# A cap of three on the loads under way at the start of a fused attention, MLP and expert kernel

## The chip, the cores and the metric

The kernel runs on one core of one Trainium2 chip. The metric is the device time of one execution in microseconds (us). TensorE (PE in the profile, with PEld for its weight loads) does the matmuls, VectorE (DVE), ScalarE (ACT) and GpSimd (POOL) the elementwise work, and SyncE (SP) issues nearly all transfers. The transfers of the core run on 16 DMA engines.

## The reference, cut to what matters

Three stages follow each other on an input of 2 sequences of 768 tokens and 8 heads of 64. The first is a decayed linear attention ("retention"), which carries a 64 by 64 state per head from block to block.

```python
def _attn_ref(q, k, v, lam):
    ...
    for b in range(nb):
        ...
        intra = np.einsum('bhic,bhjc->bhij', qb, kb) * Dmask[None]
        intra = np.einsum('bhij,bhjd->bhid', intra, vb)
        inter = np.einsum('bhid,bhde->bhie', qb * lam_pow[None], kv_state)
        out[:, :, sl] = intra + inter
        ...
        kv_state = lam_block[None, :, None, None] * kv_state + np.einsum('bhsd,bhse->bhde', kb_dec, vb)

def _moe_ref(x, g_ln, w_ch1, w_ch2):
    ...
    xn = (x - mu) / np.sqrt(var + 1e-06) * g_ln
    ch = np.maximum(xn @ w_ch1, 0.0) @ w_ch2
    return (x + ch).astype(np.float32)
```

The last stage is a mixture of 4 experts: each is a causal softmax attention with one head of 64, and each token keeps its two best. The layer norm and MLP (512 to 2048 and back) work on 1536 tokens, and so does the last stage. All inputs are float32.

## The kernel before, in words

The retention stage takes the 2 sequences in 12 chunks of 128 tokens. Chunk `n` needs two loads of 512 KB each: `qk` (q and k, transposed, `load_qk`, line 119) and `kvn` (k and v, `load_kv`, line 128). Every fourth chunk's loads go into a borrowed tile called `early`; the others rotate through three buffers, so a load also waits until the chunk that used its buffer is done. Between them the queue gets the first MLP weights, `raw`, 512 KB each (`load_w`, line 139; one of them goes to `early` too).

PE's order in this stage is written by hand. For each chunk it runs, in this order: the scores of the next chunk (`sc`, line 340, needs that chunk's `qk`), the old state's part of the output (`po<-qd,st`, line 385), the state update (`ps`, line 375, needs `kvn` and its decayed copy `kd`), and the inner part of the output (`po<-a,kvn`, line 392). DVE multiplies the scores by the decay (`a`, line 361) and sums the state (`st`); POOL makes `qd`, `kd` and `old`; ACT copies the output to `xT`. From the third chunk on, pieces of the layer norm (`mu`, `mean`, `dq`, `xn`), of weight splitting (`mag`, `top`, `w`) and later of the MLP (`h`, line 514) are put between. After the twelfth chunk the kernel is a long row of MLP and attention matmuls.

SP issues the transfers in program order, one queue, and an issue that waits holds up all issues behind it. Transfers take turns over eight semaphores. Before the change a load waits only for its buffer and for the transfer eight places in front of it, whose semaphore it takes over.

The profile's DMA queue q8, of kind "instruction", carries packets that are not loads of the kernel: 28 of them, 0.46 MB.

Of the kernel before, what the change touches and what calls it, by code (L numbers as in the profile page):

```python
# [11 lines left out]
I32 = mybir.dt.int32  # L12
# [19 lines left out]

W_SLOTS = ((4, 6), (4, 8))
WARM = (10, 3)

ROOM = (1.5, 3.0)
ROOM_MLP = 1.5
# [31 lines left out]
def model(ctx, tc, qkT, kv, lam, g_ln, w12, wat, out):  # L69
    nc = tc.nc  # L70
# [19 lines left out]
    def ps_big(name):  # L90
        return psum.tile([P, 2, 512], F32, tag="big", bufs=2, name=name)
# [10 lines left out]
    def warm(n, name):  # L102
        ps = ps_mid(f"warm{name}")
        for _ in range(n):
            nc.tensor.matmul(ps, zeros[:, :P], zeros, start=True, stop=True)

    warm(WARM[0], "a")

    R = {}

    early = xnp.tile([P, 3, 1024], F32, tag="xn", name="early")

    def load_qk(n):
        b, c = order[n]
        if n % 4 == 3:
            qk = early[:, 0].rearrange("p (a h i) -> p a h i", a=2, h=HP)
        else:
            qk = r2.tile([P, 2, HP, P], F32, tag="qk", name=f"qk{b}{c}", bufs=3)
        nc.sync.dma_start(qk, qkT[b, c])
        R.setdefault((b, c), {})["qk"] = qk  # L120

    def load_kv(n):
        b, c = order[n]
        if n % 4 == 3:
            kvn = early[:, 1].rearrange("p (a h d) -> p a h d", a=2, h=H)
        else:
            kvn = r2.tile([P, 2, H, D], F32, tag="kvn", name=f"kvn{b}{c}", bufs=3)
        nc.sync.dma_start(kvn, kv[b, c])
        R.setdefault((b, c), {})["kvn"] = kvn

    RAW = {}

    def load_w(ft, i):

        if (ft, i) == (2, 0):
            raw = early[:, 2].bitcast(I32).rearrange("p (c two) -> p c two", two=2)
        else:
            raw = stage.tile([P, 512, 2], I32, tag="raw", name=f"raw{ft}_{i}")
        nc.sync.dma_start(raw, w12[ft, :, i * 512:(i + 1) * 512].bitcast(I32)
                          .rearrange("p (c two) -> p c two", two=2))  # L140
        RAW[ft, i] = raw

    WRAW = []
# [43 lines left out]
    while rest:  # L187
        for p in rest:
            ft, i = p
# [5 lines left out]
        else:  # L195
            p = None
# [5 lines left out]
        assert n < len(steps), rest  # L202
    pieces = first + [plan[n] for n in sorted(plan)]
    to_load = [lambda p=p: load_w(*p) for p in pieces] + [lambda i=i: load_wa(i) for i in range(4)]

    def load_next(k=1):
# [76 lines left out]
    for k in (0, 1):  # L283
        load_qk(k)
    load_kv(0)
    g_sb = const.tile([P, KT], F32, tag="g", name="g_sb")
    nc.scalar.dma_start(g_sb, g_ln)
# [20 lines left out]
    for h in range(H):  # L308
        nc.vector.tensor_tensor_scan(dec[:, h, :], lq[:, h:h + 1].to_broadcast([P, P]), hit, 0.0, ALU.mult, ALU.add)
    load_kv(1)  # L310
    load_qk(2)
    load_next()
    load_kv(2)
    load_qk(3)

    for h2 in range(2):
# [18 lines left out]
    def ret_scores(n):  # L335
        r = R[order[n]]
        sc = r["sc"] = ps_big(f"sc{n}")
        for hp, h2 in HEADS:
            for kh in range(2):
                nc.tensor.matmul(sc[half(kh), h2, cols(hp)], r["qk"][half(h2), 1, hp, half(kh)],  # L340
                                 r["qk"][half(h2), 0, hp, :], start=True, stop=True, skip_group_check=True)

    def ret_qd(n):
        b, c = order[n]
        if c > 0:
            r = R[b, c]
            r["qd"] = r2.tile([P, HP, P], F32, tag="qd", name=f"qd{n}")
            nc.gpsimd.tensor_tensor(r["qd"], r["qk"][:, 0], qpow, ALU.mult)

    def ret_decay(n):  # L350
        b, c = order[n]
        r = R[b, c]
        if c < NC - 1:
# [14 lines left out]
    def ret_state(n):  # L368

        b, c = order[n]  # L370
        r = R[b, c]
        if c < NC - 1:
# [5 lines left out]
    def ret_outer(n):  # L378
        b, c = order[n]
        r = R[b, c]  # L380
        r["po"] = ps_big(f"po{n}")
        if c > 0:
            st = ST.pop(n - 1)
            for hp, h2 in HEADS:
                nc.tensor.matmul(out_at(r["po"], hp, h2), st[half(h2), hp, :], r["qd"][half(h2), hp, :],
                                 start=(hp < 2), stop=False, skip_group_check=True)
# [253 lines left out]
    while n < len(order) or min(norm_at) < 3 or norm_parts or weight_parts:  # L640
        if n < len(order):
# [8 lines left out]
            if n == 0:  # L650
                warm(WARM[1], "b")
            ret_outer(n)
# [276 lines left out]
    for k in range(len(items) + LAG + O_AT + 1):  # L929
        if k < len(items):  # L930
            b, t, e = items[k]
# [7 lines left out]
        i = k - 1  # L939
        if 0 <= i < len(items):  # L940
            att_c(*items[i])
        i = k - LAG
        if 0 <= i < len(items):
            att_t(*items[i])
        i = k - LAG - AV_AT
        if 0 <= i < len(items) and items[i][2] % 2 == 1 and i < len(items) - 1:
            b, t, e = items[i]
# [3 lines left out]
        i = k - LAG - O_AT  # L951
# [56 lines left out]
```

## Time and profile before

| what | value |
|---|---|
| median of 3 runs | 467.2 us (466.13 to 467.33) |
| profiled execution, time | 466.95 us |
| its span, first to last instruction | 465.2 us |
| PE busy | 453.3 us, 97% of the span |
| PE's granted clock | full in every slice |
| DMA, mean over the span | 91 GB/s |
| DMA in the second slice of 40 (11.6 to 23.3 us) | 409 GB/s, busy share 9 tenths or more |

The span is what the trace covers; the 1.75 us between it and the profiled time lie around it. An engine's busy time counts its own instructions; idle time before an instruction is given with what ended it.

### The profile page before, as it was taken

What the parts mean: (1) busy time and instruction counts of PE and PEld (TensorE: products, weight loads), DVE (VectorE), ACT (ScalarE), POOL (GpSimd) and SP (SyncE); (2) the same over time, 40 slices, a digit from 0 to 9 for tenths busy, and PEclk for the clock granted to TensorE, in tenths of its full rate; (3) what the DMA queues carried; (4) which work ended last, traced back from release to release, by engine and by line L of the source; (5) the groups of instructions that cost most, each with busy time, mean ns of one, the idle gap of its engine ahead of it and who ended that gap; (6) DMA issues with size and microseconds to landing.
All of it is one profiled execution on the core that took longest, in us unless ns stands there. A gap on an engine that the chain in (4) does not pass through costs nothing.

```text
span 465.2 us, 9098 instructions
## 1 busy us (share of the span) xinstructions
PE 453.3 (97%) x3562; PEld 421.0 (91%) x3563; DVE 334.6 (72%) x698; ACT 208.5 (45%) x476; POOL 86.6 (19%) x132
## 2 busy tenths in 40 slices
PE   8789999999999999999999999999999999999997
PEld 4666779999999999999999999999998898998885
DVE  5887988869778778537789745646788686586663
ACT  3568675445433213113225311311466666557673
POOL 6745500000000000000000000000055443344340
PEclk9999999999999999999999999999999999999999
DMA  7997115634421222101224412220000000001011
GB/s 281 409 359 269 48 61 190 197 90 135 138 91 50 87 92 77 60 0 47 90 92 129 155 35 51 56 65 1 0 1 0 25 25 24 23 2 38 33 45 70
DMA packets 15226, 42.33 MB, mean 91 GB/s; under 512 B 2240, under 2 KB 5072, under 8 KB 15184
## 3 DMA queue, kind: packets, MB, share of 16 engines
q1 hardware_dynamic: 14896, 41.62, 26.3%
q8 instruction: 28, 0.46, 0.4%
q10 hardware_dynamic: 288, 0.13, 0.1%
q14 instruction: 14, 0.11, 0.1%
HBM read 35.43 MB, written 6.32 MB: 90 GB/s over the span
## 4 chain that ended last, share of the span: by engine, by line
PE 73%; DVE 8%; ACT 3%; issue 1%; POOL 0%; ACTq 0%; DVEq 0%
PE y L548 27%; PE h L514 23%; PE s L844 5%; PE av L893 4%; PE t L881 4%; PE o L914 4%; PE pj L764 3%; PE pv L786 3%; DVE qs L772 1%; PE yf L570 1%; DVE kl L776 1%; DVE w L255 1%; ACT att L856 1%; DVE xn L454 0%; ACT xn L451 0%
## 5 line engine op out<-in xcount | busy, mean ns | idle before, releaser
L514 PE MATMUL h<-xn,w 128*128 128x384 f32 x768 | 139.8, 336 | 0.0
L514 PEld LDWEIGHTS h<-xn,w 128*128 128x128 f32 x768 | 133.4, 188 | 2.8 <-issue 0.8
L548 PE MATMUL y<-hs,w 128*128 128x384 f32 x552 | 99.7, 334 | 0.0
L548 PEld LDWEIGHTS y<-hs,w 128*128 128x128 f32 x552 | 96.1, 188 | 0.0
L533 ACT ACTIVATE hs<-h 128x384 fp32r<-128x384 f32 x50 | 24.5, 490 | 108.6 <-PE h L514 99.0
L778 POOL TENSOR_SCALAR kh<-kh 64x384 fp32r<-64x384 f32 x16 | 8.1, 507 | 293.1 <-ACT kh L775 291.3
L534 DVE SCALAR_TENSOR_TENSOR hs<-h,hs 128x384 fp32r<-128x384 f32 x50 | 27.7, 554 | 34.6 <-ACT hs L533 34.5
L871 POOL TENSOR_SCALAR att<-att,c,gw 128x128 f32<-128x128 f32 (+5 forms) x48 | 35.6, 747 | 51.9 <-DVE c L868 16.0
L556 DVE TENSOR_TENSOR xT<-xT,y 128x768 f32<-128x768 f32 x24 | 22.8, 951 | 28.3 <-PE y L548 28.3
L243 ACT CAST w<-top 128x512 fp32r<-128x512 f32 x32 | 19.9, 621 | 42.3 <-DVE top L237 42.3
L764 PE MATMUL pj<-x,wa 128*128 128x384 f32 x192 | 35.0, 337 | 0.0
L764 PEld LDWEIGHTS pj<-x,wa 128*128 128x128 f32 x192 | 33.3, 188 | 0.0
L882 ACT COPY aT<-t 128x512 f32<-128x512 f32 (+3 forms) x64 | 26.5, 441 | 11.2 <-PE t L881 11.0
L881 PE MATMUL t<-ident,att 128*128 128x128 f32 x168 | 26.2, 275 | 0.5 <-DVE qs L772 0.5
L252 DVE TENSOR_TENSOR top<-top,w 128x512 f32<-128x512 f32 x32 | 24.0, 750 | 0.0
L893 PE MATMUL av<-aT,v 128*64 128x128 f32 x336 | 23.7, 280 | 0.0
L844 PE MATMUL s<-kh,qs 128*128 128x512 f32 (+3 forms) x64 | 23.3, 365 | 0.0
L248 DVE SCALAR_TENSOR_TENSOR mag<-raw,mag 128x512 f32<-128x512 uint32 x31 | 22.6, 729 | 0.7
L237 DVE SCALAR_TENSOR_TENSOR top<-raw,mag 128x512 int32<-128x512 int32 x31 | 22.2, 718 | 0.5
L228 ACT ACTIVATE mag<-raw 128x512 f32<-128x512 f32 x31 | 20.5, 669 | 4.2 <-DVE w L255 2.1
L255 DVE TENSOR_TENSOR w<-top,mag 128x512 fp32r<-128x512 f32 x32 | 21.9, 684 | 0.4
L893 PEld LDWEIGHTS av<-aT,v 128*64 128x64 f32 x336 | 18.0, 136 | 4.2 <-issue 3.5
(137 smaller groups left out, 702.1 us busy)
## 6 DMA issues: line engine op xcount, KB each, us to landing
raw<-in_w SPq DMA_DIRECT2D x31, 512.0 KB, 3.7
qk<-in_qkT SPq DMA_DIRECT2D x9, 512.0 KB, 6.5
kvn<-in_kv SPq DMA_DIRECT2D x9, 512.0 KB, 6.7
xd<-xT SPq DMA_DIRECT2D x4, 768.0 KB, 4.4
xr<-xd SPq DMA_DIRECT2D x8, 384.0 KB, 3.2
out<-os SPq DMA_DIRECT2D x11, 256.0 KB, 2.0
early<-in_qkT SPq DMA_DIRECT2D x3, 512.0 KB, 8.6
early<-in_kv SPq DMA_DIRECT2D x3, 512.0 KB, 4.6
```

The source lines that it names most:

```text
L252: nc.vector.tensor_tensor(t["top"], t["top"], t["w"][:, 0].bitcast(F32), ALU.subtract)
L255: nc.vector.tensor_tensor(t["w"][:, 1], t["top"], t["mag"], ALU.add)
L514: nc.tensor.matmul(ph[:, :TB], w[:, wi, k, :], xn[:, xi, k, :], start=(i == 0), stop=(i == 11))
L533: LAST.append((nc.scalar.activation(h[:, 0], ph[:, :TB], AF.Relu), nc.vector.scalar_tensor_tensor(h[:, 1], ph[:, :TB], 0.0, h[:, 0].bitcas ...
L534: nc.vector.scalar_tensor_tensor(h[:, 1], ph[:, :TB], 0.0, h[:, 0].bitcast(F32), ALU.max, ALU.subtract)))
L548: nc.tensor.matmul(y[:, j, :TB], w[:, wi, e * P:(e + 1) * P], h[:, xi], start=(f == 0 and i == 0), stop=(f == GF - 1 and i == 2))
L764: nc.tensor.matmul(ps[:, :TB], w[:, wi, k, :], x2[:, xi, k, :], start=(i == 0), stop=(i == 11))
L844: nc.tensor.matmul(ps[:, c0:c1], q, kk[:, e, c0:c1], start=(i == 0), stop=(i == 1))
L871: nc.gpsimd.tensor_scalar(a[:, :n], a[:, :n], c, gw, ALU.mult, ALU.mult)
L881: nc.tensor.transpose(pt[:, (j - j0) * P:(j - j0 + 1) * P], a[:, j * P:(j + 1) * P], ident)
L882: nc.scalar.copy(aT[:, j0 * P:j1 * P], pt[:, :(j1 - j0) * P])
L893: nc.tensor.matmul(pav[e2 * HD:(e2 + 1) * HD, pr * P:(pr + 1) * P], v[:, j, e * HD:(e + 1) * HD], row["aT"][e][:, j * P:(j + 1) * P], star ...
```

## The change

`load_qk` and `load_kv` issue through a new function `load`, and so does `load_w` while fewer than 28 loads have gone through it. `load` keeps the issued loads in a list; from the fourth on, each gets a dependency on the one three places in front of it, so SP waits for that one's landing before it issues.

```diff
+IN_FLIGHT = 3
+N_HELD = 28
...
+    FLYING = []
+
+    def load(dst, src):
+
+        t = nc.sync.dma_start(dst, src)
+        if len(FLYING) >= IN_FLIGHT:
+            tc.add_manual_dep(t.ins, FLYING[-IN_FLIGHT].name,
+                              mybir.DependencyInfo(mybir.DependencyClass.Sync, mybir.DependencyReason.DATA),
+                              reason="in flight")
+        FLYING.append(t.ins)
...
-        nc.sync.dma_start(qk, qkT[b, c])
+        load(qk, qkT[b, c])
...
-        nc.sync.dma_start(kvn, kv[b, c])
+        load(kvn, kv[b, c])
...
-        nc.sync.dma_start(raw, w12[ft, :, i * 512:(i + 1) * 512].bitcast(I32)
-                          .rearrange("p (c two) -> p c two", two=2))
+        (load if len(FLYING) < N_HELD else nc.sync.dma_start)(
+            raw, w12[ft, :, i * 512:(i + 1) * 512].bitcast(I32).rearrange("p (c two) -> p c two", two=2))
```

No instruction moves on any engine; only SP's waits change. Here are SP's issues from the fifth instruction on, before the change. The number after a tile's name is its buffer; a wait on `DMAHW2` is one for the transfer that used that semaphore last.

```order
4 L128 DMA kvn_117<-in_kv 128x1024
5 L128 DMA kvn_154<-in_kv 128x1024
6 L119 DMA qk_156<-in_qkT 128x1024
7 L139 DMA raw_0_158<-in_w 128x1024
8 L128 DMA kvn_160<-in_kv 128x1024 [waits DMAHW0_49]
9 L119 DMA early<-in_qkT 128x1024 [waits DMAHW1_49]
10 L128 DMA early<-in_kv 128x1024 [waits DMAHW2_49]
11 L119 DMA qk_203<-in_qkT 128x1024 [waits DMAHW3_49,PE_49]
12 L128 DMA kvn_263<-in_kv 128x1024 [waits PE_49,DMAHW4_49,Activation_49,Pool_49]
13 L119 DMA qk_265<-in_qkT 128x1024 [waits DMAHW5_49,Pool_49]
```

The first nine transfers wait for nothing that takes long; the tenth (number 10) waits for the first `qk`, eight places in front. The same issues after the change:

```order
4 L116 DMA kvn_117<-in_kv 128x1024
5 L116 DMA kvn_154<-in_kv 128x1024 [waits DMAHW2_49]
6 L116 DMA qk_156<-in_qkT 128x1024 [waits DMAHW3_49]
7 L116 DMA raw_0_158<-in_w 128x1024 [waits DMAHW4_49]
8 L116 DMA kvn_160<-in_kv 128x1024 [waits DMAHW5_49,DMAHW0_49]
9 L116 DMA early<-in_qkT 128x1024 [waits DMAHW6_49,DMAHW1_49]
10 L116 DMA early<-in_kv 128x1024 [waits DMAHW7_49]
11 L116 DMA qk_203<-in_qkT 128x1024 [waits DMAHW0_49,PE_49]
12 L116 DMA kvn_263<-in_kv 128x1024 [waits PE_49,DMAHW1_49,Activation_49,Pool_49]
13 L116 DMA qk_265<-in_qkT 128x1024 [waits DMAHW2_49,Pool_49]
```

Number 5 now waits for number 2, number 6 for number 3, and so on up to the 29th load, number 31; the waits for buffers (PE, ACT, POOL) stay. Numbers 2 to 4 go out as before. In what follows "load 9" means the load with that number.

## Rows read from the trace of the kernel before

**Rows 1.** Page: busy time by engine, and the instruction queue's packets, MB, share.

```profile
PE 453.3 (97%) x3562; PEld 421.0 (91%) x3563; DVE 334.6 (72%) x698; ACT 208.5 (45%) x476; POOL 86.6 (19%) x132
...
q8 instruction: 28, 0.46, 0.4%
```

**Rows 2.** Windows of 6 us: busy per engine (count), PE clock, DMA share, GB/s.

```profile
6.00:12.00 6.00, 5.38 (x130) 4.17 (x127) 3.85 (x6) 2.73 (x9) 4.80 (x8) 1.00 1.03 414
...
24.00:30.00 6.00, 6.00 (x133) 4.31 (x136) 3.83 (x7) 3.28 (x8) 3.86 (x4) 1.00 1.00 375
```

**Rows 3.** Timeline of SP, 0 to 45 us: start, duration, issue.

```profile
1.19 0.88 SPq L119 DMA_DIRECT2D qk<-in_qkT  x2
...
4.90 0.45 SPq L119 DMA_DIRECT2D early<-in_qkT  x1
5.81 0.33 SPq L128 DMA_DIRECT2D early<-in_kv  x1
7.17 0.33 SPq L119 DMA_DIRECT2D qk<-in_qkT  x1
...
16.43 0.43 SPq L139 DMA_DIRECT2D early<-in_w  x1
```

**Rows 4.** DMA issues from 4.95 to 5.30 us: count, KB, us to landing.

```profile
early<-in_qkT SPq DMA_DIRECT2D x1, 512.0 KB, 9.9
```

**Rows 5.** DMA issues from 7.20 to 7.40 us.

```profile
qk<-in_qkT SPq DMA_DIRECT2D x1, 512.0 KB, 11.5
```

**Rows 6.** DMA issues from 16.45 to 16.80 us.

```profile
early<-in_w SPq DMA_DIRECT2D x1, 512.0 KB, 10.0
```

**Rows 7.** Timeline of PE, 5.7 to 36.5 us; last, idle time before and its releaser.

```profile
5.84 1.10 PE L340 MATMUL sc<-qk 64*64 64x128 f32 x32 [0.23 <-DMA qk<-in_qkT]
...
11.07 1.10 PE L340 MATMUL sc<-qk 64*64 64x128 f32 x32 [0.23 <-DMA qk<-in_qkT]
...
14.90 1.10 PE L340 MATMUL sc<-early 64*64 64x128 f32 x32 [0.61 <-DMA early<-in_qkT]
...
19.73 1.10 PE L340 MATMUL sc<-qk 64*64 64x128 f32 x32
...
25.12 1.10 PE L340 MATMUL sc<-qk 64*64 64x128 f32 x32
...
32.04 1.10 PE L340 MATMUL sc<-early 64*64 64x128 f32 x32 [0.55 <-DVE a L361]
```

**Rows 8.** Timeline of PEld, 13 to 25 us.

```profile
17.61 0.46 PEld L385 LDWEIGHTS po<-qd,st 64*64 64x64 f32 x16 [1.85 <-issue]
...
23.97 0.19 PEld L392 LDWEIGHTS po<-a,early 128*64 128x64 f32 x2 [0.97 <-issue]
```

**Rows 9.** Windows cut at PE's stalls and at q8's packets; columns as Rows 2.

```profile
0.00:9.80 9.80, 8.00 (x93) 3.99 (x96) 5.47 (x11) 2.43 (x6) 6.29 (x26) 1.00 0.73 257
9.80:15.01 5.21, 4.37 (x105) 3.61 (x104) 3.09 (x5) 3.90 (x12) 4.54 (x6) 1.00 1.03 409
15.01:17.42 2.41, 0.99 (x32) 0.75 (x31) 2.38 (x3) 0.74 (x3) 1.53 (x2) 1.00 1.02 410
...
21.53:23.96 2.43, 1.61 (x38) 1.32 (x30) 2.43 (x4) 0.31 (x2) 1.56 (x2) 1.00 0.99 396
...
100.62:125.38 24.76, 24.76 (x144) 24.76 (x143) 20.39 (x41) 11.92 (x21) 0.00 (x0) 1.00 0.38 120
```

**Rows 10.** DMA queues from 15.00 to 15.02 us: packets, MB, share.

```profile
q8 instruction: 1, 0.02, 312.5%
```

**Rows 11.** DMA queues from 21.50 to 21.55 us.

```profile
q8 instruction: 1, 0.02, 136.8%
```

**Rows 12.** DMA queues from 100.60 to 100.65 us.

```profile
q8 instruction: 1, 0.02, 118.2%
```

**Rows 13.** Timeline of all engines, 0 to 75 us: two rows on the fourth chunk.

```profile
17.01 1.21 DVE L361 TENSOR_TENSOR a<-sc,dec 128x1024 f32<-128x1024 f32 x1
...
17.54 0.73 POOL L358 TENSOR_TENSOR kd<-early,dec 128x320 f32<-128x320 f32 x1 [1.00 <-DMA early<-in_kv]
```

**Rows 14.** Tile `raw`, 100 to 400 us: us to landing, least, median, most.

```profile
DMA to landing us min/median/max: 3.4/3.7/4.1
```

## The prediction

> **What bounds the kernel now.** I read the page first. PE is busy for 453.3 of 465.2 us [rows 1], so at most 12 us of PE's idle time can be won in the whole kernel, and whatever makes PE's row of work start or move on earlier by some time brings the end forward by that time, as long as nothing else steps in. The change touches only the first 29 loads, which the windows place in the first 42 us. There the DMA engines are full: a share of 1.03 and 414 GB/s from 6 to 12 us, still 1.00 from 24 to 30 [rows 2].
>
> Next I put issues and landings together. Load 9 (`early`, the fourth chunk's `qk`) is issued at 4.90 and takes 9.9 us, so it lands at 14.8; load 11 is issued at 7.17 and lands 11.5 later, at 18.7; load 17 is issued at 16.43 and lands at 26.4 [rows 3 to 6]. From load 11 to load 17 that is 7.7 us for six loads, 1.28 us each: loads land in the order of their issue at the full rate, and one that is issued early only waits longer. From 9 to 11, though, two loads took 3.9 us, 1.3 more than their share. Load 10 is the late one: POOL, which waits for it, starts at 17.54 [rows 13], 2.7 us after load 9 landed.
>
> Then PE's own stalls. Before 24 us it has two kinds of them. The scores `sc` wait for loads: at 5.84, 11.07 and 14.90 [rows 7], 0.2 to 0.6 us each. And at 17.61 and 23.97 PE's weight loads start after 1.85 and 0.97 us of idle time that the profile puts down to "issue" [rows 8], that is to nothing it sees. I take these two for waits for instructions. The instruction queue moved 28 packets of 0.46/28 MB, 16 KB each [rows 1]; PE ran 3562 + 3563 instructions, 254 per packet, so one packet is a block of about 254 PE instructions. A packet started at 15.0, another at 21.5 [rows 10, 11]. After the first PE ran 63 instructions up to its stall, after the second 68 [rows 9]; each time the stall ended about 2.5 us after the packet's start (17.42 and 23.96). In the quiet part a packet started at 100.6 [rows 12], and PE ran 287 instructions without idle time up to 125.4 [rows 9]. So a fetch that has DMA engines to itself comes a whole block ahead, and one behind a queue of loads comes late. The block that stalled at 17.42 was preceded by one that began about 254 instructions earlier, at 9.8 us (189 instructions by then). If its fetch was asked for there, it lay 5.2 us behind the loads; the second, from 17.42 to 21.5, 4.1 us.
>
> **The change, part by part.** *The new waits on SP.* Up to eight loads were under way, now three. Does the rate hold? No row shows three in flight at this place, so I bound it. A load alone takes 3.7 us from issue to landing [rows 14]; SP issued load 10 at once when load 2 landed at about 5.8 (5.81 against PE's start at 5.84) [rows 3, 7], so a turn is about 3.75 us. Three loads per turn are 1.25 us each, under the 1.28 that the engines take: cost 0. That is the low end. The high end is the very first load, 1.19 to 5.8, 4.6 us [rows 3, 7]: 1.55 us each, 0.27 lost per load. I take the low end, because the three that are queued keep the engines fed, as with the 3.7 us loads, while the first load starts from nothing. Behind a waiting issue on SP stand only further loads in this stretch, and whoever waits for those is counted with the loads.
>
> *The loads that now go out later.* Load 9 leaves when load 6 lands (about 11.0, when `sc` starts [rows 7]) and not at 4.90, but lands in the same turn. Nothing that PE waits for comes sooner either: the first three loads, which start PE, go out as before.
>
> *The fetch at 15.0.* With at most three loads in front, each 1.28 us, it can lie at most 3.8 us behind its request, and by the share of the waits before (5.2 us where six loads were under way, 0.87 us per load) about 2.6 us. It then starts at 9.8 + 2.6 = 12.4, at the latest 13.6, and its block is there 2.4 us later (as 15.0 to 17.42), at 14.8 to 16.0. PE's 63 instructions end about 16.0 (`sc` at 14.90 plus 1.10). So the stall goes. But the fetch takes its engine from the loads: before, it made load 10 late by 1.3 us, and now it comes in front of load 9, for which PE waits. I put that whole 1.3 us on load 9: `sc` starts at 16.2 and not 14.90, ends at 17.3, and line 385 follows at 17.3 where it was 17.61. Gain: 0.3 us, not 1.6. The decay product `a`, at 17.01 before [rows 13], starts at 17.3 and ends at 18.5, in time for the next `sc`, which goes from 19.73 to 19.4 and has its load 11 at 18.7.
>
> *The fetch at 21.5.* Its request moves to 17.1; 2.6 to 3.8 us behind it starts by 20.9, and 2.4 us later, at 22.1 to 23.3, the block is there. PE reaches it at 23.96 - 0.97 - 0.3 = 22.7. I take the stall as gone but for the late end: gain 1.0 us. After that the PE rows up to 30 us have no wait that ends on a load; loads land 3 to 4 us before use (`sc` at 32.04 waits for DVE, 0.55 us [rows 7], and DVE hangs on PE's rows). Later fetches caused no stall.
>
> The sum is 0.3 + 1.0 = 1.3 us, from the profiled 466.95: 465.65. The median of the runs shown, 467.2, is 0.25 above the profiled time, so 465.7 is 0.3% under it.
>
> [...]
>
> **The rivals.**
>
> *Both stalls go and load 9 is not delayed.* If the early fetch falls on a DMA engine that is ahead of the others, load 9 still lands at 14.8. Then line 385 starts at 16.0, but the next `sc` is bound by load 11 at 18.7 instead of 19.73: 1.0 us, and with the second stall 2.0. Time 464.95. For it: the fetch at 21.5 delayed no load (1.28 each up to load 17). Against it: the one at 15.0 did.
>
> *The fetch does not come sooner.* Its lateness may not come from the loads queued in front but from what each engine holds already, and three loads may hold as much of that as seven. Waits of 5.2 us with six under way and 4.1 with about seven do not grow in step with the queue, which speaks for it; the quiet fetch at 100.6 speaks against it. Stalls then stay and the time is 467.0, the profiled one. [...]
>
> *The turn gets longer, and the kernel slower.* A load lands with the slowest of 16 engines. A fetch holds one engine, and where a deep queue let the others run on, now all wait for the next issue, so each fetch adds its 1.3 us to the turn. Place: `sc` at 32.04, whose load 19 goes out five turns after load 4. Load 4 lands at about 8.4 (two loads of 1.28 after 5.8), so load 19 lands at 8.4 plus five turns, and that meets 32.04 at a turn of 4.7 us. Below that nothing is lost; at 5.1 load 19 lands at 33.9, 1.9 us late: 468.9. One fetch per turn on 3.75 would give 5.05, but they come every 6 us or so. Slack against it, 3 us at this place, is what speaks most for no loss.
>
> **How the numbers follow.** A difference under 0.3%, 1.4 us, is about what a measurement of this kernel cannot tell from no change; that is 465.8 and below for faster, 468.6 and above for slower. Chances: forecast 0.45, with its own range 465.1 to 466.4; both stalls without delay 0.14; no sooner fetch 0.28; longer turn 0.13. The forecast lies on the edge, and I count a little over six tenths of it as faster: 0.28 + 0.14 + 0.02 from fetches late in the start, 0.44. Same: 0.17 + 0.26 = 0.43. Slower: 0.13. The range leaves out most of the longer turn and a tenth of the quick case: 464.7 to 467.8.
>
> **What would show each step.** The rate: from load 5 to load 17 still about 1.28 us per landing, and windows from 6 to 24 us near 1.00 of DMA share. The fetches: q8's first packet at 12 to 13.6 us, the second by 21. PE: no "issue" idle time over 0.3 us before 25 us, and line 340's fourth start at 16.2 with a wait for `early`. The start at 25.12 moves to about 23.8, and all later PE rows by the same 1.3 us. Wrong I would be if the packets of q8 still start 4 to 5 us after PE enters a block, if `sc` at 11.07 is already later by more than 0.3 us (the turn is longer than 3.75), or if PE gets its 1.3 us early and gives it back at 32 to 47 us, where DVE is the one it waits for.

## The result: slower by 0.7%

The changed kernel takes 470.12 us (median of 6 runs, 468.85 to 471.49) where the kernel before takes 467.13 (6 runs on the same chip, 466.13 to 467.33): a ratio of 1.0068, 95% interval 1.0048 to 1.0088. The forecast was 465.7. The profiled execution took 470.68 us, its span is 468.9, 3.7 more than before.

Line numbers are 12 higher than before (`sc` is L352, the loads all have L116). First the page of after, busy time by engine; it answers to [rows 1]:

```profile
PE 455.6 (97%) x3563; PEld 423.7 (90%) x3563; DVE 334.7 (71%) x698; ACT 208.7 (45%) x476; POOL 85.8 (18%) x132
```

PE is busy 2.3 us longer with the same matmuls, so of the 3.7 us 2.3 are matmuls that ran slower and 1.4 are more idle time. Next the windows of after, columns as in [rows 2]; the last one covers 24 us:

```profile
6.00:12.00 6.00, 5.78 (x131) 4.68 (x131) 3.86 (x6) 2.73 (x9) 4.79 (x8) 1.00 0.96 345
12.00:18.00 6.00, 2.29 (x56) 1.77 (x48) 3.67 (x5) 3.12 (x9) 2.74 (x3) 0.93 0.90 320
18.00:24.00 6.00, 5.81 (x88) 5.18 (x92) 3.00 (x5) 0.99 (x4) 3.31 (x4) 0.50 0.76 250
24.00:30.00 6.00, 5.86 (x154) 4.50 (x151) 4.16 (x6) 3.93 (x11) 4.49 (x4) 1.00 0.98 333
...
6.00:30.00 24.00, 19.74 (x413) 16.14 (x415) 14.69 (x21) 10.77 (x31) 15.32 (x17) 0.86 0.90 312
```

Two columns matter. The last two show the DMA engines at a share of 0.76 to 0.98 and 250 to 345 GB/s, where [rows 2] had 1.00 and more. The same 24 us of the kernel before:

```profile
6.00:30.00 24.00, 20.04 (x468) 15.59 (x469) 18.46 (x25) 11.85 (x34) 16.81 (x19) 1.00 1.02 402
```

90 GB/s less over 24 us is 2.2 MB, four loads that have not arrived by 30 us. And PE's clock (third from the end) is 0.50 from 18 to 24, where before it was full in every slice. It fell while PE stood still for almost 4 us: it is 1.00 from 14.29 to 17.15 and 0.50 from 17.15 to 18.19, with PE busy for 0.00 us in both.

The timeline of SP in after, answering to [rows 3]: each issue now marks the landing of the load three places in front.

```profile
7.11 0.33 SPq L116 DMA_DIRECT2D qk<-in_qkT  x1
8.39 0.33 SPq L116 DMA_DIRECT2D raw<-in_w  x1
9.74 0.33 SPq L116 DMA_DIRECT2D kvn<-in_kv  x1
11.00 0.33 SPq L116 DMA_DIRECT2D early<-in_qkT  x1
14.04 0.33 SPq L116 DMA_DIRECT2D early<-in_kv  x1
...
18.14 0.33 SPq L116 DMA_DIRECT2D kvn<-in_kv  x1
19.37 0.33 SPq L116 DMA_DIRECT2D qk<-in_qkT  x1
...
32.50 0.33 SPq L116 DMA_DIRECT2D early<-in_kv  x1
```

These are loads 6 to 10, 12, 13 and 20. Up to load 9 all goes as forecast: load 6 took 3.9 us (7.11 to 11.00), and load 9 leaves at 11.00. But load 10, which waits for load 7, leaves at 14.04: load 7 took 5.65 us, not 3.75. Load 9 itself takes 7.1 us and lands at 18.1, where it landed at 14.8 before. From load 6 to load 13 it is 12.26 us for seven loads, 1.75 each. So three under way kept the rate at first and then no longer, as two more windows of after show:

```profile
6.00:9.75 3.75, 3.75 (x83) 2.93 (x85) 3.31 (x5) 0.90 (x4) 2.54 (x5) 1.00 1.03 419
9.75:13.50 3.75, 3.53 (x92) 2.98 (x90) 1.78 (x3) 1.86 (x6) 3.23 (x4) 1.00 0.88 227
```

In the second the engines are busy nine tenths of the time and move little more than half the bytes.

What PE makes of it, in the timeline of PE, last column the idle time before and its releaser (answers to [rows 7]):

```profile
11.07 1.10 PE L352 MATMUL sc<-qk 64*64 64x128 f32 x32 [0.22 <-DMA qk<-in_qkT]
18.19 1.98 PE L352 MATMUL sc<-early 64*64 64x128 f32 x32 [3.90 <-DMA early<-in_qkT]
23.71 1.21 PE L352 MATMUL sc<-qk 64*64 64x128 f32 x32
...
35.07 1.10 PE L352 MATMUL sc<-early 64*64 64x128 f32 x32 [0.77 <-DMA early<-in_qkT]
39.71 1.10 PE L352 MATMUL sc<-qk 64*64 64x128 f32 x32 [1.09 <-DVE xn L466]
...
57.26 1.10 PE L352 MATMUL sc<-early 64*64 64x128 f32 x32
```

At 18.19 PE is 3.3 us late and the same 32 matmuls take 1.98 us instead of 1.10. Without the stall that stood at 17.4 before, it would be 1.6 us late at the next step, but the slower clock takes 2.3 until 23.71 (before: 19.73), 4.0 late. At 35.07 it waits for load 19. The row at 39.71 names `xn`, but load 21, the `qk` it needs, was issued at 33.7 and took 5.8, so it landed just then too. At 57.26 PE is 3.4 us late, near the 3.7 of the span; the row of the kernel before, last start of `sc`:

```profile
53.81 1.10 PE L340 MATMUL sc<-early 64*64 64x128 f32 x32
```

The two stalls of [rows 8] are gone; on the weight loads the largest "issue" idle time from 19 to 30 us is 0.36 us. But the first packet of the instruction queue came no sooner. After, DMA queues from 14.90 to 14.95 us (before, [rows 10]: from 15.00):

```profile
q8 instruction: 1, 0.02, 123.4%
```

It starts at 14.93. The stall is gone because PE itself reached the place only at 19.7. It is also the first packet of that queue after the start, so the long turn of load 7, over at 14.04, is not the work of a fetch.

### The profile page after: what moved, and what is told of

Read it like the earlier page. It is cut to its first block, busy times and chain, and to the rows that moved or that the text cites. A ratio compares the mean times of both kernels' runs of the same rounds, so it can differ in the third digit from the quotient of the medians.

```text
span 468.9 us, 9097 instructions
## 1 busy us (share of the span) xinstructions
PE 455.6 (97%) x3563; PEld 423.7 (90%) x3563; DVE 334.7 (71%) x698; ACT 208.7 (45%) x476; POOL 85.8 (18%) x132
## 4 chain that ended last, share of the span: by engine, by line
PE 73%; DVE 8%; ACT 3%; issue 1%; POOL 0%; ACTq 0%; DVEq 0%
PE y L560 27%; PE h L526 23%; PE s L856 4%; PE av L905 4%; PE t L893 4%; PE o L926 4%; PE pj L776 3%; PE pv L798 3%; DVE qs L784 1%; PE yf L582 1%; DVE kl L788 1%; DVE w L267 1%; ACT att L868 1%; DVE xn L466 0%; ACT xn L463 0%
```

## The experiments

Two theories stood against each other: that the loads' rate is what costs (three under way don't keep the engines fed), and that PE's slower clock after one long wait is what costs. A third question was whether the fetch really comes sooner with fewer loads queued, and where that gain goes. Ratios are to the kernel before on the same chip, and of mean times, so they need not be those of the medians; the last start of `sc`, 53.81 before, shows how late PE is when the stage ends.

### How many loads under way

```diff
-IN_FLIGHT = 3
+IN_FLIGHT = 2      (and 4, 5, 6, 1)
```

> Cap of two instead of three. Theory A (a load takes about 5.1 us from issue to landing when it is issued late into running engines, so a cap of n gives one landing per 5.1/n us and never less than 1.28): landings 2.3 to 2.6 us apart, load 9 at about 20 us, the score matmul that waits for load 19 at 42 to 44 us (32.0 before), time 476 to 482 us. Theory B (the loss at a cap of three is a one-off delay at load 9, and the loads after it have slack): load 9 some 2 us later than with three, nothing more, 471 to 473 us.

> Cap of four. [...] If the instruction fetch also comes sooner with fewer loads in front (theory F), the idle times before 17.4 and 24 us shrink and the time is 465.5 to 466.5 us. If an engine holds about four loads ahead of a fetch whatever is queued behind them (theory G), the fetch starts at 15.0 as before and the time is 466.8 to 467.8 us.

> Cap of five. Theory A: full rate, load 9 at 14.8. Theory F: fetch a little sooner than before, time 466 to 467 us. Theory G: everything as before, fetch at 15.0, both idle times stay, 467.0 to 467.4 us.

> Cap of six. All theories: nearly the kernel before, 466.8 to 467.4 us; it shows what the cap does where it hardly binds.

> One load under way at a time, so each turn is measured with nothing else of the loads on the engines. With two under way a load took some 4.6 us, with three some 5.1 to 5.6, a lone one in the quiet part 3.7. Theory Q (a load's turn grows with what lies on the engines with it, from a fixed part of well over 2 us): loads land one per about 3.7 us here too, load 9 at about 5.8 + 7 x 3.7 = 32, and the rate over the stretch is about 140 GB/s. Theory P (the start of the kernel is a slow place for any load, whatever else is queued): a lone load takes some 5 us here as well, load 9 lands at about 41, and the rate is about 105 GB/s. In both the kernel is slower by tens of us, since 28 loads take 28 turns (some 104 us by Q, 140 us by P, against 42 now), and the first retention chunks wait for each.

| cap | median us | ratio, 95% interval | us per load, 6 to 13 | GB/s, 6 to 30 us |
|---|---|---|---|---|
| 1 | 514.21 | 1.1032 [1.0986, 1.1077] | 3.28 | 156 |
| 2 | 480.12 | 1.0298 [1.0275, 1.0321] | 2.36 | 242 |
| 3 (the change) | 470.12 | 1.0068 [1.0048, 1.0088] | 1.75 | 312 |
| 4 | 466.99 | 1.0003 [0.9988, 1.0018] | 1.29 | 373 |
| 5 | 466.54 | 1.0002 [0.9986, 1.0018] | | 409 |
| 6 | 466.57 | 1.0000 [0.9988, 1.0013] | | 404 |

The fourth column comes from SP's timeline, as above: the issues of loads 6 and 13, seven loads apart. The third row shown is the issue of load 20. Cap 1, SP, and then its window of 24 us:

```profile
15.35 0.33 SPq L116 DMA_DIRECT2D qk<-in_qkT  x1
...
38.30 0.33 SPq L116 DMA_DIRECT2D qk<-in_qkT  x1
...
62.19 0.33 SPq L116 DMA_DIRECT2D early<-in_kv  x1
```

```profile
6.00:30.00 24.00, 11.60 (x191) 9.05 (x187) 7.08 (x11) 5.74 (x17) 8.43 (x11) 0.77 0.49 156
```

Cap 2, the same two views:

```profile
9.10 0.33 SPq L116 DMA_DIRECT2D qk<-in_qkT  x1
...
25.64 0.33 SPq L116 DMA_DIRECT2D qk<-in_qkT  x1
...
40.12 0.33 SPq L116 DMA_DIRECT2D early<-in_kv  x1
```

```profile
6.00:30.00 24.00, 16.62 (x329) 13.95 (x327) 12.76 (x18) 8.61 (x26) 12.09 (x15) 0.82 0.75 242
```

Cap 4:

```profile
5.82 0.33 SPq L116 DMA_DIRECT2D qk<-in_qkT  x1
...
14.84 0.33 SPq L116 DMA_DIRECT2D qk<-in_qkT  x1
...
25.79 0.33 SPq L116 DMA_DIRECT2D early<-in_kv  x1
```

```profile
6.00:30.00 24.00, 21.03 (x453) 16.38 (x453) 18.05 (x24) 11.83 (x34) 15.22 (x17) 0.93 0.99 373
```

Multiplied by the cap, the time per load is the mean turn, from issue to landing: 3.28, 4.73, 5.25 and 5.15 us. It depends on the stretch: from load 6 to load 20 the loads are 3.35, 2.22, 1.81 and 1.43 us apart, which makes the turns 3.35, 4.43, 5.44 and 5.71. A load by itself takes 3.28 us at this busy place, close to the 3.7 of [rows 14]; so the place is not slow, and it is the company of other loads that lengthens the turn. With four the engines are full up to 18 us (408 GB/s from 12 to 18; 4 times 1.28 is 5.1), and not quite after it (337 GB/s from 18 to 24). With three the turn is about as long, though the engines have gaps. Cap 6 has the same added waits on SP and costs nothing, so it is the number under way that costs, not the waits as such. Share and rate also say how long the engines work on one load of 524 thousand bytes: 0.49 x 524/156 = 1.65 us alone, 1.51 with three, 1.02 x 524/402 = 1.33 in the kernel before. So with fewer loads under way the engines took longer for the same bytes.

Cap 2 came out as theory A has it for rate and load 9 (landed at 19.5), and so did cap 4, for which its 5.1/n gives 1.28 us per load (measured 1.29; load 9 landed at 14.8). Cap 1 lies near theory Q (3.28 us per load, 3.7 expected) and far from theory P. Cap 5 lies in theory F's range and cap 6 0.2 us under its own, both the kernel before within the noise. Theory F's time for cap 4 missed too: the first fetch starts at 14.89, the first stall stays, and 466.99 us is theory G's. With cap 4 PE's clock did not stay full: its mean was 0.97 from 12 to 18 us and 0.74 from 18 to 24, where the kernel before has 1.00 in both. First the row of the kernel before at the first stall, then cap 4's:

```profile
17.65 0.67 PE L385 MATMUL po<-qd,st 64*64 64x128 f32 x16 [1.64 <-DVE top L237]
```

```profile
17.66 1.13 PE L397 MATMUL po<-qd,st 64*64 64x128 f32 x16 [1.64 <-DVE top L249]
```

After the same wait of 1.64 us the same 16 matmuls took 0.67 us before and 1.13 with cap 4, whose fifth scores then started at 21.33 (before: 19.73).

From cap 4 up the time is that of the kernel before, though with caps 4 and 5 the second stall goes. Cap 5, timeline of PE:

```profile
36.89 0.48 PE L352 MATMUL sc<-qk 64*64 64x128 f32 x9 [1.10 <-issue]
47.08 1.10 PE L352 MATMUL sc<-qk 64*64 64x128 f32 x32 [0.99 <-DVE a L373]
53.78 1.10 PE L352 MATMUL sc<-early 64*64 64x128 f32 x32
```

Its second fetch starts at 20.39 (21.53 before), and PE is 1.1 us early at 24 us. A later fetch then comes too late: at 36.89 `sc` breaks off for 1.10 us, a stall that the kernel before has not; at 43.06 the tenth scores start where they did before (43.11). At 47 us PE waits for DVE, as it does in the kernel before (1.00 us at 47.14), and the last `sc` stands at 53.78, the old place.

### The cap on the early or on the later loads alone

```diff
-        if len(FLYING) >= IN_FLIGHT:
+        if IN_FLIGHT <= len(FLYING) <= 9:      (early: loads 5 to 11)
+        if len(FLYING) >= 10:                  (late: from load 12 on)
```

> The cap of three holds only for loads 5 to 11; later ones wait as before the change. Theory E (the loss is PE's wait for load 9 and what follows from it): load 9 at 18 us, PE idle 3.9 us, its clock falls as with the full change, PE 2.8 us late at the sixth scores (25.1 before); the waits for loads 19 and 21 that the full change shows (0.7 and 1.0 us) are gone; time 468.5 to 469.5 us. Theory L (the loss is made by the later loads): 466.5 to 467.3 us.

> The cap of three holds only from load 12 on. Theory E: load 9 at 14.8 us and the clock full there; loads from 12 on land up to 1.7 us apart instead of 1.28, load 19 at 30 to 33 us, scores at 32.0 up to 1 us late; time 467.0 to 468.2 us. Theory L: 469.5 to 470.5 us.

Early: 469.49 us (468.63 to 470.72), ratio 1.0060 [1.0041, 1.0080]. Late: 467.89 (466.88 to 471.0), ratio 1.0038 [1.0019, 1.0057]. Early, timeline of PE:

```profile
17.53 1.10 PE L352 MATMUL sc<-early 64*64 64x128 f32 x32 [2.32 <-DMA early<-in_qkT]
21.35 1.10 PE L352 MATMUL sc<-qk 64*64 64x128 f32 x32 [0.79 <-DMA qk<-in_qkT]
...
34.46 1.10 PE L352 MATMUL sc<-early 64*64 64x128 f32 x32 [1.13 <-DVE xn L466]
...
40.62 0.48 PE L352 MATMUL sc<-qk 64*64 64x128 f32 x9 [1.98 <-issue]
...
57.49 1.10 PE L352 MATMUL sc<-early 64*64 64x128 f32 x32
```

In early PE's clock stays full (1.00 in every window from 6 to 70 us) and every whole `sc` of the rows above takes 1.10 us. Yet at 34.46 PE is 2.4 us late (before: 32.04), where the whole change is 3.0 late: load 19 landed at 34.3 here, though the row names `xn`. So most of the loss stands without the slow clock. Three of early's four executions had a mean granted clock of 0.999 or 1.0 and took 468.63 to 470.72 us; all six of the whole change had 0.991 to 0.996. The last `sc` starts at 57.49, 3.7 late, but part of that is another stall: at 40.62 `sc` breaks off for 1.98 us, which it does not in the whole change, and the profiled execution, 470.72 us, is the slowest of the four. Seven capped loads are enough for most of the loss (0.60% of 0.68%), because the engines are full afterwards (407 to 410 GB/s from 30 to 42 us, no more than the 409 to 414 of the kernel before up to 24 us), so that the lost time was not made up. Theory E's time holds, at its edge, but the fall of the clock and the end of the wait for load 19, which it expected too, did not come. Late, timeline of PE:

```profile
32.79 1.10 PE L352 MATMUL sc<-early 64*64 64x128 f32 x32 [1.90 <-DMA early<-in_qkT]
...
53.77 1.10 PE L352 MATMUL sc<-early 64*64 64x128 f32 x32
```

In late the rate falls too (231 GB/s from 18 to 24 us), and PE waits 1.90 us for load 19. But its second fetch started at 18.60 and the second stall was gone, so that in this profile the two cancel. The median of its runs, within theory E's range, is 0.9 us above that profiled execution. The slower executions are those with a lower clock: five of the ten, the profiled one among them, had a mean granted clock of 0.999 or 1.0 and took 466.88 to 467.65 us, the other five, at 0.993 to 0.996, took 468.12 to 471.0. The two parts sum to 0.98%, more than the whole change, but with intervals of some 0.2% to either side of each number the excess is not clear of noise.

### The clock kept up

17 matmuls of zeros ahead of the fourth scores fill PE's wait; their result is not used.

```diff
-WARM = (10, 3)
+WARM = (10, 3, 17)
...
+            if n == 2:
+                warm(WARM[2], "c")
```

> The full change, and 17 matmuls of zeros (0.21 us each, 3.7 us) put on PE in front of the scores that wait for load 9, so that PE is not idle there; nothing else is changed, their result is not used. [...] Theory O (only the wait itself costs): time stays at 469.5 to 470.5 us.

471.2 us (469.75 to 473.31), ratio 1.0107 [1.0079, 1.0134]. Timeline of PE:

```profile
19.01 1.10 PE L352 MATMUL sc<-early 64*64 64x128 f32 x32 [0.31 <-DMA early<-in_qkT]
21.97 1.10 PE L352 MATMUL sc<-qk 64*64 64x128 f32 x32
...
36.77 1.99 PE L352 MATMUL sc<-early 64*64 64x128 f32 x32 [3.63 <-DMA early<-in_qkT]
...
60.04 1.10 PE L352 MATMUL sc<-early 64*64 64x128 f32 x32
```

The clock was kept there (1.00 from 6 to 30 us), and PE was 1.7 us ahead of the changed kernel at 21.97. It only got to the next wait sooner: 3.63 us for load 19, and the clock fell in its turn (0.50 from 36 to 42 us). Load 19 also came 1.7 us later than in the changed kernel (36.77, there 35.07), and why is open; but at 35.07 too PE would have stood no earlier than the changed kernel did. The time lies above theory O's range, and above the 467.8 us that an estimate from the changed kernel gives if its slow clock is what costs (470.12 less the 2.3 us that the slower clock took there), with an interval that overlaps that of the whole change, and the profiled execution, 473.31 us, is the slowest of the four. So the theory that the one slow stretch from 18 to 24 us is what costs falls: PE runs into the loads wherever they are, and the slower matmuls of the changed kernel fill time that would be waited. That a lower clock costs nothing at all is not shown, and late's executions speak against it.

### Two caps, and weights outside the cap

mix holds five under way up to load 12, then four; rawfree caps `qk` and `kvn` at three and lets `raw` go freely.

```diff
+        cap = 5 if len(FLYING) <= 10 else 4                       (mix)
...
-        (load if len(FLYING) < N_HELD else nc.sync.dma_start)(
+        nc.sync.dma_start(                                        (rawfree)
```

> A cap of five up to load 12 and of four after it, meant to keep the rate and let the later instruction fetches come sooner. Theory F (PE's idle time before 24 us goes and no other takes its place): 465.3 to 466.3 us. Theory S (what PE wins there is given back before 43 us, where in all kernels with a cap of five or more the tenth scores begin at 43.1 us): 466.4 to 467.3 us.

> Cap of three on the qk and kvn loads alone; the weight loads are issued as before, on top of it, so that three or four loads are under way. Theory B: a rate between those of caps of three and four while a weight load is under way; load 9 at 15.5 to 17 us, PE idle before it 1.2 to 2.7 us, time 467.3 to 469.3 us. If a weight load is itself what makes the turn long (load 7 took 5.6 us in the full change), load 9 lands at 18 us as with the full change, 469.5 to 470.5 us.

mix: 466.92 us (466.37 to 467.2), ratio 1.0007 [0.9998, 1.0015]. Timeline of PE:

```profile
36.70 0.48 PE L353 MATMUL sc<-qk 64*64 64x128 f32 x9 [0.59 <-issue]
...
46.99 1.10 PE L353 MATMUL sc<-qk 64*64 64x128 f32 x32 [1.08 <-DVE a L374]
53.67 1.10 PE L353 MATMUL sc<-early 64*64 64x128 f32 x32
```

As with cap 5, the time gained early (1.5 us at the sixth scores, 23.58, before 25.12) is gone but for 0.15 us by 47 us, to waits for DVE (0.36 us at 27.82, 0.44 at 35.23) and to a later fetch; theory S holds. No version was found that beats the kernel before. rawfree: 468.04 us (467.35 to 470.89), ratio 1.0035 [1.0020, 1.0051], between caps 3 and 4, as its window is:

```profile
6.00:30.00 24.00, 20.02 (x428) 15.63 (x424) 16.07 (x23) 11.35 (x33) 15.32 (x17) 0.93 0.98 358
```

Load 9 lands at 15.67, as theory B has it, and the first stall stays (its fetch starts at 15.93).

### Halves of loads

Does the number of loads under way count, or their bytes? Each held load became two of 64 partitions, with six halves under way (half6), or held by no cap (halffree).

```diff
-        t = nc.sync.dma_start(dst, src)
+        for rows in (slice(0, 64), slice(64, 128)):
+            t = nc.sync.dma_start(dst[rows], src[rows])
...
-IN_FLIGHT = 3
+IN_FLIGHT = 6          (halffree: 1000)
```

> Each held load split into two of 64 partitions (256 KB), cap of six halves: the bytes under way are those of a cap of three. Theory B (the rate is bytes under way over the turn, and a half's turn is hardly shorter): landings of whole loads 1.6 to 1.75 us apart, load 9 at 17 to 18.5 us, time 469 to 471 us. Theory N (six transfers under way, refilled in smaller steps, keep the engines fed): 1.28 to 1.4 us apart, load 9 at 14.8 to 15.7 us, time 466.5 to 467.8 us.

> The same halves without a cap; the eight semaphores then hold eight halves under way, the bytes of four whole loads. Theory B: as a cap of four, load 9 at 14.8 to 15.2 us, time 466.5 to 467.5 us. Theory N: the same. If halves themselves cost (more issues on SP, 0.33 us each), the rate would fall under that of a cap of four and load 9 would land after 15.5 us.

483.07 us (482.3 to 483.94), ratio 1.0359 [1.0340, 1.0377], and 485.25 (484.51 to 486.22), 1.0400 [1.0380, 1.0421]. The window of half6, then that of halffree:

```profile
6.00:30.00 24.00, 16.83 (x286) 13.23 (x287) 10.63 (x16) 7.53 (x23) 11.09 (x14) 0.79 1.04 230
```

```profile
6.00:30.00 24.00, 15.44 (x286) 12.21 (x287) 10.50 (x16) 7.68 (x23) 10.96 (x14) 0.86 1.04 231
```

Theories B and N missed in both runs; only the last sentence of the second expectation came true, that halves themselves cost, and not for the reason that it gives, SP's issues. The engines are full, at a share of 1.04, and move only 230 GB/s, cap or no cap: the halves are the cost, and the pair says nothing on the question it was made for, which stays open.

## Why the prediction was wrong, step by step

**The rate, "cost 0" under the new waits on SP.** This is the step that failed. It took a turn of about 3.75 us, the turn of a lone load, and divided it by three: 1.25 us per load. The reason it gave, that "the three that are queued keep the engines fed", held up to 9.75 us (419 GB/s, load 6 in 3.9 us) and no longer: then the rate fell to 227 GB/s and load 7 took 5.65. The mean turn with three under way is 5.25 us, 1.75 per load, above even the high end of 1.55. The caps of 1 to 4 show why the division was wrong: the turn grew with what was under way (3.28, 4.73 and 5.25 us with one, two and three). A lone load's 3.7 us and the one load issued at 5.8 said nothing about three that share the engines.

**The fetch at 15.0, to start at 12.4 to 13.6.** Wrong: 14.93, 5.2 us after PE began that block, as before. The wait does depend on the queue, but not in proportion. The same fetch waits about 5.0 to 5.2 us with four or more under way, 1.6 with two, 1.4 with one; with three it was 5.2, 2.7 (early) and 5.9 (warm17), and with rawfree's three or four 6.2. So the wait goes with the loads under way, but only a cap that starves the engines shortens it with any certainty.

**Load 9 late by 1.3 us, `sc` at 16.2.** Mis-sized: 18.19, late by 3.3, since the rate was lost and not only a fetch's place.

**Both stalls gone, worth 1.3 us in sum.** The stalls went, and with them 1.6 and 1.0 us of idle time, but the first not for the reason forecast: its fetch came no sooner, PE came later. That they are waits for instructions is borne out: counting every record of PE in the trace (matmuls, weight loads, waits on semaphores), the two stalls of the kernel before and their like in caps 4 to 6, early, late, mix and rawfree all stand at number 448, 704 or 1216, or one further, which are steps of 256. But in the changed kernel PE was late for another reason by more than that.

**The second fetch by 20.9.** It started at 20.94, which is luck: PE entered that block at 19.7 and not at 17.1, and the fetch came 1.2 us after that, not 2.6 to 3.8. In the capped kernels that stay fed (4, 5, mix) it started about 1 to 2.5 us sooner than before. The gain of 1 to 1.5 us that cap 5 and mix have from it is real at 24 us, down to 0.8 and 0.5 us by 35 and all but gone by 47, the case named last in the prediction, though DVE has a part in it with mix alone and with cap 5 it is a later stall for a fetch.

**The rival that the turn gets longer** is what happened, and its price was about right: it gave 468.9 at a turn of 5.1. Its mechanism was not: it made each fetch lengthen the turn, and held that nothing is lost before load 19, with 3 us of slack there. Cap 1 has the same fetches and turns of 3.28, and load 7's long turn was over before the first fetch began. The rival's premise, that a load lands with the slowest engine, fits the trace of the kernel before: load 9's semaphore has 16 updates from 14.22 to 14.76 us, load 10's has 16 from 15.50 to 17.38, and POOL, which waits for load 10, starts at 17.54. And the first loss is at load 9, where the prediction had seen no slack at all; I priced the rival at the far load and not at the near one. The sign that was to show a longer turn, `sc` at 11.07 coming later, was blind to it in the profile of after: load 6 still lands on time, and load 7 is the first late one. In early and warm17, which are the same kernel up to there, that `sc` started at 12.19 and 11.89; a landing can move by a microsecond from one execution to the next, and one profile does not show it.

**Left open:** why the turn grows as it does, so that three under way leave gaps where four fill the engines up to 18 us; why the engines work longer on the same bytes in a thin queue; and how much of the 3 us the lower clock costs by itself.

## What to carry to other kernels

A load's time alone, divided by the number under way, is no rate: the turn grew in company (3.28 us alone, 5.25 with three under way), so read the rate from a stretch with that many under way, or measure a row of caps. Where DMA engines are full and a stage waits for its loads, ask what a gap in them costs. Here it was paid where it was longer than the slack of the next load that is waited for: over the 24 us cap 4 moved 29 GB/s less than the kernel before and lost no time, the cap of three 90 GB/s less and lost 3 us. An idle time that goes away is no gain until the end of the stage stands earlier; look there, not at the stall.

## What the runs showed of the hardware

- Loads of 64 partitions moved 230 GB/s with the engines full (share 1.04), loads of 128 partitions 402 at 1.02.
- PE's granted clock went from 1.00 to 0.50 at 17.15 us, 2.9 us into a wait of 3.90, and the same 32 matmuls took 1.98 instead of 1.10 us; with early, a wait of 2.32 us left it at full. With cap 4 it had a mean of 0.74 from 18 to 24 us, where a wait of 1.64 us ends at 17.66; with the same wait the kernel before has 1.00, so the length of the one wait does not settle it.
- A load that alone takes 3.28 us took, in the mean of loads 6 to 13, 4.73 with two under way, 5.25 with three and 5.15 with four.
